# Inputs of the second filter group kept in the filter's buffers, and weight tiles rounded in two halves

## The chip, the cores and the metric

The kernel runs on one core of a Trainium2 chip. The metric is the device time of one execution in microseconds (us); less is better. A core has TensorE (PE, matrix products), VectorE (DVE), ScalarE (ACT) and GpSimd (POOL), which compute, and SyncE (SP), which only issues DMAs here. Each takes its instructions in order: one that waits holds up all that stand behind it on the same engine. DMAs are issued by SP, ACT and POOL.

## The reference

Eight sequences x of 3008 rows and 256 channels go through a filter along the sequence, and its result through a mixer:

```
y  = irfft(rfft(x, axis=1) * (filt_r + 1j * filt_i), n=3008, axis=1)   # float32
h  = relu(y^T @ w_tok1) @ w_tok2            # over the sequence, 256 wide
u  = y + h^T
out = u + relu(u @ w_ch1) @ w_ch2           # over the channels, 1536 wide
```

The mixer's four weights arrive as float64. [...]

## The kernel before

The sequence is split as 3008 = 64 x 47, so that the filter's transforms are matrix products. The batches go in groups: 0, then (1, 2), (3, 4), (5, 6), and 7. For a group, the generator `dft` (line 443) makes first its A units (`a_unit`, line 432): an input of 128 partitions by two rows of 256 is multiplied by a table on PE, ACT copies the result to a tile t1 (two buffers), and ACT issues the DMA that writes it to z in DRAM. The second group has 24 such units, 12 a batch. Each input x comes by two DMAs (`x_load`, line 412) into the pool xp, which has two buffers (XB = 2), so an input is asked for two units ahead. After the A units come the B units (`b_unit`, line 488, and `bi_unit`, line 512): z is read back, multiplied by a table on PE, by the filter on DVE (lines 506 to 510) and by another table on PE. The filter lies in three buffers `filts` (128 x 1024 float32 each), which `filt_load` fills two chunks ahead; they are set to zero once, at the start (line 885), since some of their partitions are never loaded. The generator yields between its steps, and whoever calls `next` decides what stands beside each step.

Rounding. There are 40 weight tiles: 12 of w_tok1, 16 of w_tok2, two early ones of w_ch1 (tiles 28 and 29), and ten late ones, tiles 30 to 39, in the order of LAST (line 373): wc2 0, wc1 1, wc1 4, wc2 1, wc1 2, wc2 2, wc1 5, wc2 3, wc2 4, wc2 5. A tile passes through three steps: its load, by SP or POOL (`begin`); a copy with a factor on ACT (line 250, `copy`); and four DVE operations (lines 252, 253, 255, 257) and the sum of both parts (line 278, `end`). A wc2 tile, and the second wc1 tile of two, is then combined on POOL (`combine`, lines 337 to 344): five operations for a channel pair, the last of which (line 344) writes the form s4. `convert` (line 389) ends one tile, starts the copy of the next, and has POOL issue loads for tiles further on. So ACT's copy is always one tile ahead of DVE.

The mixer (`mix`, line 799) goes through 36 passes for each batch: six blocks m of the sequence by six channel pairs jp. I number the passes of batch 0 from 0. Products of 2 x 2 blocks are made with seven products and extra sums in place of eight products. A pass stands in this order: `convert`; `up_first` (four products on PE, line 693, and a copy s on ACT, line 696); `up_middle` (two DVE sums); the three sums of the pair before (`h_sums`, DVE); `down` part 0 of the pair before (PE, line 727); a yield, place 0, where a step of the filter may stand; `convert`; `up_last` (three products on PE, line 709, then two DVE sums hh, each with a RELU on ACT, line 714); a yield, place 1; `down` part 1; a yield, place 2. All DVE sums of the mixer go through line 671. `up_first` writes the PSUM banks that `up_last`'s sums of the pass before read, so it waits for them. `down` of channel pair jp is made one pass after its `up_last` and needs the combined wc2 tile jp; `up_first` of jp needs the combined wc1 tiles.

The order before pass 0 is written out at lines 886 to 932: batch 0's filter, with the first 12 tiles beside it; then tiles 12 to 27, with two A units of the second group among them; `token_sums(0)` (96 products, line 570); `token_relu`; tiles 28 and 29, each with a `u_unit` (lines 600 and 592); `v_steps`; two more A units; then pass 0. In batch 0 every place takes an A unit until they are all done (20 of them); from then on 35 steps are spread over 48 of the places 1 and 2 (lines 940 to 956). The ten late tiles end in passes 0 to 4, two a pass.

Of the kernel before, what the change touches and what calls it, by code (L numbers as in the profile page):

```python
# [32 lines left out]
XB = 2  # L33
KC = 2
# [90 lines left out]
def kernel(  # L125
# [116 lines left out]
    def halves(st, n, pair):  # L242

        words = [st.bitcast(t).rearrange("p (n w) -> p n w", w=2)[:, 0:n] for t in (U32, FP32)]
        lo, hi, hi_f = words[0][:, :, 0], words[0][:, :, 1], words[1][:, :, 1]
        top, rest = (v[:, 0:n] for v in pair)
        top_i, rest_i = top.bitcast(U32), rest.bitcast(U32)


        nc.scalar.activation(out=top, in_=hi_f, func=AF.Copy, scale=2.0 ** -112)  # L250
        yield
        nc.vector.tensor_scalar(out=top_i, in0=top_i, scalar1=3, scalar2=None, op0=ALU.logical_shift_left)
        nc.vector.scalar_tensor_tensor(out=top_i, in0=hi, scalar=0x80000000, in1=top_i,
                                       op0=ALU.bitwise_and, op1=ALU.bitwise_or)
# [13 lines left out]
    def rounded(st, n, parts, late):  # L268
        if late:

            pair = (p1p.tile([P, 512], FP32, tag="p1", name="top"), p2p.tile([P, 512], FP32, tag="p2", name="rest"))
        else:
            pair = spare_pair()
        h = halves(st, n, pair)
        yield next(h)
        top, rest = next(h)
        for src, dst in parts:
            nc.vector.tensor_tensor(out=dst, in0=src(top), in1=src(rest), op=ALU.add)
# [17 lines left out]
    def w1_load(i):  # L296
# [14 lines left out]
        yield next(h)  # L311
        on_chip(wai_t, *next(h), 512, [(lambda v: v, w1[:, 2 * i:2 * i + 2, :].rearrange("p a t -> p (a t)"))])

    def w2_load(i):
# [15 lines left out]
        if i < BY_PE:  # L330
            h = halves(st, n + more, spare_pair())
            yield next(h)
# [45 lines left out]
    begin, copy, end = iter(tiles), iter(tiles), iter(tiles)  # L378
# [10 lines left out]
    def convert():  # L389

        ended[0] += 1
        while behind and behind[0][0] < ended[0] - 2:
            behind.pop(0)[1]()
        advance(end)
        advance(copy)
        fill(6)
# [13 lines left out]
    xs = {}  # L410

    def x_load(b, c):
# [30 lines left out]
    def dft(bs):  # L443
# [15 lines left out]

        ahead = NXC if first else XB  # L460
        for u in todo[0:ahead]:
            x_load(*u)
        if not first:
            yield True
        for i, u in enumerate(todo):
# [5 lines left out]
            if i + ahead < len(todo):  # L471
                x_load(*todo[i + ahead])
# [57 lines left out]

        for c in range(2):
            t2_load(c)
            if not first:
                w_load(c)
# [264 lines left out]
    def mix(next_ready):  # L799
# [9 lines left out]


# [20 lines left out]
        for i in range(len(items) + 1):  # L831
            now, old = i < len(items), i >= 1
            convert()
            if now:
# [7 lines left out]
                up_middle(hhs[i], w, g, s)  # L842
            one_step()
# [37 lines left out]
    with tc.manual_schedule():  # L881
# [105 lines left out]
```

## Time and profile before

| | |
|---|---|
| four executions | 2570.22, 2571.33, 2572.34, 2575.5 us; median 2571.84 |
| the profiled execution | 2570.22 us, span in the trace 2568.4 us |
| PE busy | 2487.5 us, 97% of the span |
| DVE busy | 1945.3 us, 76% |
| ACT, POOL busy | 660.2 us (26%), 578.0 us (23%) |
| HBM | 168.96 MB read, 77.22 MB written, 96 GB/s over the span |

Where what lies, in us from the start of the span: batch 0's filter ends at about 106; `token_sums(0)` runs from 122.4 to 143.2; pass 0 begins on PE at 154.1 and pass 5 at 212.4; the last A unit of the second group is at 226.8 and its first B unit at 241.8.

How to read the rows: a row of a timeline has the start, the length, the engine, the line of the kernel, the operation, the tile written and the tiles read, the shape, the number of instructions merged into it, and in brackets the idle time of the engine ahead of it with what ended it. The engine ACTq, SPq or POOLq is the part of an engine that issues DMAs. A row of windows has the stretch, its length, the busy time of each engine with the number of instructions, the granted TensorE clock, the DMA engines' share and GB/s.

### The profile page before, as it was taken

Reading aid. Unit: us, or ns where it says so; the run is one execution under the profiler, and the core shown is the slowest. Engines: PE = TensorE matmul, PEld = TensorE weight load, DVE = VectorE, ACT = ScalarE, POOL = GpSimd, SP = SyncE. Lnnn points to the kernel's source line nnn. Section 1 sums busy time; section 2 is a strip of 40 time slices with the busy share of each in tenths; the row PEclk is TensorE's granted clock in tenths of the full one; section 3 lists DMA queues with packets and bytes.
Section 4 is the critical chain, followed back from the end, with each engine's and each line's share of the span. In section 5 each row is a group of like instructions: output and inputs, shape, how many; then the busy total and the mean of one; then the engine's idle time right before and its main releaser. Section 6 shows DMA issues by size and latency. Waiting matters only on the chain.

```text
span 2568.4 us, 32318 instructions
## 1 busy us (share of the span) xinstructions
PE 2487.5 (97%) x11204; PEld 2045.5 (80%) x11204; DVE 1945.3 (76%) x3668; ACT 660.2 (26%) x1312; POOL 578.0 (23%) x1051
## 2 busy tenths in 40 slices
PE   6979999999999999999999999999999999999998
PEld 3557666888888777898888777898888888898887
DVE  7997888566686998756776889856788587757776
ACT  3533222123221222212221222212222122212222
POOL 4563322212111121122121111211211121211222
PEclk8999999999999999999999999999999999999999
DMA  9874444233332332213332333213333222111100
GB/s 211 235 210 147 125 130 140 79 110 102 123 105 78 94 109 74 86 58 109 112 108 86 94 115 97 89 34 110 99 111 90 66 76 71 40 31 37 44 13 20
DMA packets 166932, 248.39 MB, mean 97 GB/s; under 512 B 35184, under 2 KB 112450, under 8 KB 166768
## 3 DMA queue, kind: packets, MB, share of 16 engines
q1 hardware_dynamic: 94176, 152.20, 19.8%
q0 software_dynamic: 32640, 46.51, 7.2%
q10 hardware_dynamic: 39952, 47.61, 5.8%
q8 instruction: 89, 1.46, 0.3%
q14 instruction: 75, 0.61, 0.1%
HBM read 168.96 MB, written 77.22 MB: 96 GB/s over the span
## 4 chain that ended last, share of the span: by engine, by line
PE 70%; DVE 17%; DMA 3%; issue 2%; ACT 2%; SPq 1%; POOL 1%; ACTq 0%; DVEq 0%; POOLq 0%
PE ps_po L727 24%; PE ps_pg L693 14%; PE ps_pg L709 10%; DVE t L671 3%; PE ps_acc L570 3%; DVE hh L671 3%; PE ps_b L614 2%; PE ps_b L570 2%; PE ps_acc L614 2%; DVE u L671 2%; DVE s L671 2%; PE ps_acc L592 2%; PE ps_b L592 2%; PE ps_acc L434 1%; PE ps_acc L518 1%
## 5 line engine op out<-in xcount | busy, mean ns | idle before, releaser
L772 POOL DMA_DIRECT2D out_dram<-r x757 | 410.5, 551 | 1779.8 <-ACT t L524 741.2
L671 DVE TENSOR_TENSOR hh<-ps_pg,s 128x512 f32<-128x512 f32 (+3 forms) x864 | 482.9, 587 | 281.9 <-ACT s L696 271.6
L714 ACT ACTIVATE hh<-hh 128x512 f32<-128x512 f32 (+1 forms) x576 | 348.0, 621 | 1179.7 <-DVE hh L671 1179.7
L727 PE MATMUL ps_po<-t,wc 128*128 128x256 f32 (+1 forms) x2304 | 535.8, 375 | 6.4 <-DVE t L671 5.4
L727 PEld LDWEIGHTS ps_po<-t,wc 128*128 128x128 f32 x2304 | 434.4, 190 | 131.9 <-issue 54.5
L693 PE MATMUL ps_pg<-v,wc 128*128 128x256 f32 (+1 forms) x1728 | 413.7, 375 | 4.1 <-DVE v L671 2.4
L727 PE MATMUL ps_po<-hh,wc 128*128 128x256 f32 (+1 forms) x1728 | 412.8, 375 | 2.1 <-POOL wc L344 1.9
L693 PEld LDWEIGHTS ps_pg<-v,wc 128*128 128x128 f32 x1728 | 326.6, 190 | 45.5 <-DVE v L671 6.4
L727 PEld LDWEIGHTS ps_po<-hh,wc 128*128 128x128 f32 x1728 | 327.7, 190 | 40.4 <-POOL wc L344 2.3
L709 PE MATMUL ps_pg<-u,wc 128*128 128x256 f32 (+1 forms) x1152 | 293.6, 377 | 5.4 <-DVE hh L671 5.1
L671 DVE TENSOR_TENSOR t<-t,hh 128x256 f32<-128x256 f32 (+1 forms) x576 | 244.5, 424 | 19.8
L709 PEld LDWEIGHTS ps_pg<-u,wc 128*128 128x128 f32 x1152 | 216.1, 190 | 42.7 <-DVE hh L671 16.4
L671 DVE TENSOR_TENSOR s<-ps_pg,hh 128x512 f32<-128x512 f32 (+1 forms) x288 | 196.1, 681 | 30.3 <-DVE hh L671 0.5
L671 DVE TENSOR_TENSOR t<-hh 128x512 f32<-128x512 f32 (+1 forms) x288 | 193.4, 672 | 0.6 <-ACT hh L714 0.6
L696 ACT COPY s<-ps_pg 128x256 f32<-128x256 f32 (+1 forms) x288 | 105.8, 367 | 340.5 <-PE ps_pg L693 325.3
L693 PE MATMUL ps_pg<-u,wc 128*128 128x256 f32 (+1 forms) x576 | 168.9, 375 | 0.8 <-DVE hh L671 0.8
L709 PE MATMUL ps_pg<-v,wc 128*128 128x256 f32 (+1 forms) x576 | 168.8, 375 | 0.0
L671 DVE TENSOR_TENSOR u<-ps_b,u 128x512 f32<-128x512 f32 (+3 forms) x111 | 63.5, 572 | 99.5 <-PE ps_b L614 81.0
L671 DVE TENSOR_TENSOR u<-ps_acc,u 128x512 f32<-128x512 f32 (+3 forms) x99 | 57.4, 579 | 95.4 <-PE ps_acc L614 79.2
L693 PEld LDWEIGHTS ps_pg<-u,wc 128*128 128x128 f32 x576 | 109.1, 190 | 23.8 <-issue 10.0
L709 PEld LDWEIGHTS ps_pg<-v,wc 128*128 128x128 f32 x576 | 108.7, 190 | 13.1
L518 PE MATMUL ps_acc<-p,wb 128*96 128x256 f32 (+1 forms) x256 | 97.3, 481 | 12.3 <-ACT t L524 4.5
(123 smaller groups left out, 2514.3 us busy)
## 6 DMA issues: line engine op xcount, KB each, us to landing
w<-w_tmp SPq DMA_DIRECT2D x35, 896.0 KB
g_tmp<-t ACTq DMA_DIRECT2D x128, 192.0 KB
out_dram<-r POOLq DMA_DIRECT2D x698, 32.0 KB, 1.8
x<-in_x_dram SPq DMA_DIRECT2D x173, 128.0 KB
z_tmp<-t ACTq DMA_DIRECT2D x84, 256.0 KB
t<-z_tmp SPq DMA_DIRECT2D x112, 192.0 KB
t<-g_tmp SPq DMA_DIRECT2D x42, 512.0 KB
wb<-wbi_t SPq DMA_DIRECT2D x80, 224.0 KB
```

What stands on the lines that cost most here:

```text
L434: nc.tensor.matmul(ps, wa0 if b == 0 else wa, xs.pop((b, c)).rearrange("p a d -> p (a d)"), start=True, stop=True)
L518: nc.tensor.matmul(ps[0:KR], wbs[k // WC][:, k % WC, P:], p, start=(i == 0), stop=(i == len(parts) - 1))
L570: nc.tensor.matmul(acc[:, t, :], w1[:, a, ts(t, P)], t4[b, a // TC4][:, a % TC4, :], start=(a == 0 and t == 0), stop=(a == A - 1 and t == ...
L592: nc.tensor.matmul(ps[:, ds(q * P, n)], t4[b, c][:, r, ts(dh, P)], wai[:, 0:n], start=(first and q == 0), stop=(not first and q == 3))
L614: nc.tensor.matmul(ps[:, ds(j * hw, hw)], h1[:, n, :], w2m[m % 2][:, at, 0:hw], start=(i < 2 and j == 0), stop=(j == len(todo) - 1))
L671: nc.vector.tensor_tensor(out=out, in0=in0, in1=in1, op=op)
L693: nc.tensor.matmul(ps[:, 0:hw], chan[0][:, jp, n, :], mov, start=True, stop=True)
L696: nc.scalar.copy(out=s[:, 0], in_=g[0][:, 0, 0:hw])
L709: nc.tensor.matmul(ps[:, 0:hw], chan[0][:, jp, n, :], mov, start=True, stop=True)
L714: nc.scalar.activation(out=hs, in_=hs, func=AF.Relu)
L727: nc.tensor.matmul(po[i][:, j, 0:hw], chan[1][:, jp, n, :], mov, start=(jp == 0 and first == 1), stop=(jp == JP - 1 and last == 1))
L772: q.dma_start(rows[g, e, :, ds(h * A + 4 * m, n)], blocks[ts(g, CW), h, e, 0:n])
```

## The change

The second group's A units take their inputs from eight buffers in place of two: of each eight, the first two lie in xp and the other six in the halves of the three `filts`, which nobody uses at that time. Inputs 4 to 9 are issued by POOL, three at tile 22 and three at tile 25; each A unit then loads the next one on SP. After the last A unit POOL sets the three `filts` to zero, ahead of the filter's loads. Four A units (in place of two) stand before pass 0, and they stand right behind `token_relu`, ahead of tiles 28 and 29; two less are left for the passes.

A tile's DVE work is split: the first half is lines 252 and 253, the second lines 255 and 257 and the sum, followed by POOL's combine, the next tile's copy and the loads. Before pass 0 both halves still stand together in `convert`. In a pass, one tile's first half now stands behind `up_middle` and its second half behind `down` part 0; the next tile's first half stands behind place 0, ahead of `up_last`, and its second half behind `up_last`'s sums. `convert` is no longer called at a pass's start.

```diff
+XF = 2 * FB
...
     def halves(st, n, pair):
         nc.scalar.activation(out=top, in_=hi_f, func=AF.Copy, scale=2.0 ** -112)
         yield
         nc.vector.tensor_scalar(out=top_i, ...)
         nc.vector.scalar_tensor_tensor(out=top_i, ...)
+        yield
         nc.vector.tensor_scalar(out=rest_i, ...)
         nc.vector.scalar_tensor_tensor(out=rest, ...)
         yield top, rest
...
     def convert():
-        ended[0] += 1
-        while behind and behind[0][0] < ended[0] - 2:
+        while behind and behind[0][0] < ended[0] - 1:
             behind.pop(0)[1]()
+        advance(middle)
+        convert_end()
+
+    def convert_end():
+        ended[0] += 1
         advance(end)
         advance(copy)
         fill(6)
...
-    def x_load(b, c):
+    def x_load(b, c, i, queue=None):
...
-        t = where.tile([P, xc, dc], FP32, tag=tag, name="x")
+        j = i % (XB + XF) - XB
+        if b in GROUPS[1] and j >= 0:
+            t = filts[j // 2][:, j % 2]
+        else:
+            t = where.tile([P, xc, dc], FP32, tag=tag, name="x")
...
-            q = nc.gpsimd if b == 0 and h else nc.sync
+            q = queue or (nc.gpsimd if b == 0 and h else nc.sync)
...
+        to_load = list(enumerate(todo))
+        def more(n, queue=None):
+            for i, u in to_load[0:n]:
+                x_load(*u, i, queue)
+            del to_load[0:n]
+        more(NXC if first else XB)
+        if bs == GROUPS[1]:
+            ahead.append(more)
...
             a_unit(*u)
-            if i + ahead < len(todo):
-                x_load(*todo[i + ahead])
+            more(1)
...
+        if bs == GROUPS[1]:
+            for t in filts:
+                nc.gpsimd.memset(t, 0.0)
         for c in range(2):
             t2_load(c)
...
+        def late_half(second):
+            if ended[0] < len(tiles):
+                convert_end() if second else advance(middle)
...
         for i in range(len(items) + 1):
-            convert()
             if now:
...
                 up_middle(hhs[i], w, g, s)
+                late_half(False)
             one_step()
             if old:
...
                 down(mo, jo, 0, hhs[i - 1], tts[i - 1], pos.setdefault((bo, mo), []))
             if now:
                 u_parts(b, m, jp, 0)
+            late_half(True)
             yield b, i % n, 0
-            convert()
+            late_half(False)
             if now:
                 up_last(jp, uts[b, m], vts[b, m], w, g, s, hhs[i])
+            late_half(True)
             one_step()
...
             convert()
             if i - rounds < XB:
                 next(second)
+            if i in (A // 2 + TC * N2 // NG - 6, A // 2 + TC * N2 // NG - 3):
+                ahead[0](XF // 2, nc.gpsimd)
             if i == A // 2 + BY_PE - 1:
                 sum_up()
                 acc = token_sums(0)
         h1s[0] = token_relu(0, acc)
+        for _ in range(2 * XB):
+            next(second)
         for dh in range(DH):
             convert()
             u_part(0, 0, dh)
         for f in v_steps(0, 0):
             f()
-        for _ in range(XB):
-            next(second)
```

More of the change, by code (lines that the diff above doesn't have):

```diff
@@ L274, in rounded @@
         h = halves(st, n, pair)
+        yield next(h)
         yield next(h)
@@ L311, in w1_load @@
         yield next(h)
+        yield next(h)
         on_chip(wai_t, *next(h), 512, [(lambda v: v, w1[:, 2 * i:2 * i + 2, :].rearrange("p a t -> p (a t)"))])
@@ L331, in w2_load @@
             h = halves(st, n + more, spare_pair())
+            yield next(h)
             yield next(h)
@@ L377 @@
              + [wc1_load(c * (DC // 512), False) for c in range(DH)] + [f(i) for f, i in LAST])
-    begin, copy, end = iter(tiles), iter(tiles), iter(tiles)
+    begin, copy, middle, end = (iter(tiles) for _ in range(4))
     def advance(it):
@@ L389, in convert @@
     def convert():
+        while behind and behind[0][0] < ended[0] - 1:
+            behind.pop(0)[1]()
+        advance(middle)
+        convert_end()
+    def convert_end():
         ended[0] += 1
-        while behind and behind[0][0] < ended[0] - 2:
-            behind.pop(0)[1]()
         advance(end)
@@ L406, in start @@
         begun[0] += 1
-    xs = {}
-    def x_load(b, c):
+    xs, ahead = {}, []
+    def x_load(b, c, i, queue=None):
         where, tag = ((xp, "x"), (tp, "t"), (vp, "v"), (up, "u"), (t1p, "t1"), (t2p, "t2"))[c // 2] if b == 0 else (xp, "x")
@@ L458, in w_load @@
             filt_load(c, first)
-        ahead = NXC if first else XB
-        for u in todo[0:ahead]:
-            x_load(*u)
+        to_load = list(enumerate(todo))
[6 more added lines that the diff above has]
+            ahead.append(more)
         if not first:
```

## The prediction

> **What bounds the kernel now.** I read the page's slices first, then a table of 10 us windows, then the timelines of PE, DVE, ACT and POOL where PE is not full. In the slices TensorE is at 90% or more in all but the first and the third of 40 slices (64.2 us each); what the change can win lies between 64 and 256 us.
>
> ```profile
> PE   6979999999999999999999999999999999999998
> DVE  7997888566686998756776889856788587757776
> ```
>
> ```profile
> core 0: us, PE busy (x) PEld busy (x) DVE busy (x) ACT busy (x) POOL busy (x), PEclk, DMA share, GB/s
> ...
> 140.00:150.00 10.00, 6.52 (x29) 4.38 (x28) 9.45 (x20) 2.50 (x5) 3.78 (x8) 1.00 0.62 169
> ...
> 160.00:170.00 10.00, 8.32 (x31) 5.57 (x32) 9.07 (x16) 4.38 (x8) 9.15 (x16) 1.00 0.82 254
> 170.00:180.00 10.00, 6.59 (x25) 4.09 (x23) 9.58 (x17) 4.50 (x8) 9.43 (x15) 1.00 0.84 247
> ...
> 210.00:220.00 10.00, 10.00 (x44) 7.40 (x42) 5.42 (x11) 5.19 (x10) 1.50 (x4) 1.00 0.44 142
> ```
>
> From 120 to 210 us DVE is the full engine and PE has holes (granted clock 1.00); from 210 us PE is full and DVE half empty. Now PE's holes:
>
> ```profile
> 147.86 1.12 PE L600 MATMUL ps_acc<-w,h 128*128 128x512 f32 x2 [2.80 <-DVE w L278]
> ...
> 156.45 1.56 PE L693 MATMUL ps_pg<-v,wc 128*128 128x256 f32 x6 [1.73 <-POOL wc L343]
> 158.76 1.10 PE L434 MATMUL ps_acc<-x,wa 128*128 128x512 f32 x2 [0.74 <-DMA x<-in_x_dram]
> ...
> 163.61 1.10 PE L434 MATMUL ps_acc<-x,wa 128*128 128x512 f32 x2 [1.34 <-DMA x<-in_x_dram]
> ...
> 180.19 1.13 PE L727 MATMUL ps_po<-hh,wc 128*128 128x256 f32 x4 [1.94 <-POOL wc L344]
> ...
> 187.77 1.10 PE L434 MATMUL ps_acc<-x,wa 128*128 128x512 f32 x2 [1.71 <-DMA x<-in_x_dram]
> ```
>
> The x waits of this stretch (0.74, 1.34, 0.83, 1.71, 0.72, and 0.37 at 220.67) sum to 5.7 us; those for rounded weights (2.80, 1.73, 1.94) to 6.5. Whether they are worth that depends on DVE, whose own gaps from 155 to 208 us sum to 2.0 us (0.55 at 168.44, 0.61 at 190.89, 0.87 at 203.10). What opens and closes the gap of 0.55:
>
> ```profile
> 163.62 1.28 DVE L671 TENSOR_TENSOR hh<-ps_pg,s 128x512 f32<-128x512 f32 x2
> ...
> 167.19 0.69 DVE L278 TENSOR_TENSOR wc<-top,rest 128x512 f32<-128x512 f32 x1
> 168.44 0.42 DVE L671 TENSOR_TENSOR hh<-ps_pg,s 128x256 f32<-128x256 f32 x1 [0.55 <-ACT s L696]
> ```
>
> ```profile
> 174.50 2.04 POOL L350 DMA_DIRECT2D st<-in_moe_w_ch_dram  x4
> 176.55 0.61 POOL L340 TENSOR_SCALAR wc<-wc 128x128 f32<-128x128 f32 x1
> ...
> 179.36 0.78 POOL L344 TENSOR_TENSOR wc<-wc 128x128 f32<-128x128 f32 x1
> ```
>
> Between the last sums of a pass (hh at 163.62) and the first sums of the next (168.44) lie 4.82 us that ACT needs: two RELUs, the rounding's copy, two copies of the filter's units with their DMA issues, then the copy s. Today a whole weight tile (four operations and the sum, 3.1 to 3.6 us) and the hh sums (1.2) lie in this stretch and all but fill it.
>
> **The change, part by part.** All is counted from the profiled execution (2570.22 us, span 2568.4; 1.6 below the median 2571.84); the sum is a difference, and I add it to the median.
>
> *Filter inputs in filts.* The 24 inputs of the second group are the same DMAs. Twelve issues go to POOL (six inputs, two halves) at 0.62 each, the row of x loads on POOL: 7.4 us among POOL's waits for stage buffers at 134 to 146 us; behind them queue the last weight loads, which have slack: tile 32, issued at 144.52, is copied at 161.06. With eight inputs ahead I drop every x wait. The three memsets (nearest rows: 0.91 for 128x1024 on DVE, 0.52 for 64x512 on POOL) make about 3 us in POOL's 31.46 us of idle before 243.12; on SP the filter loads behind them wait until 231.4 for z anyway. I cost them at nothing; uncovered, 3.
>
> *Four units behind the token sums.* PE is idle from 143.24 to 147.86 but for two matmuls, so 4 x 0.88 = 3.5 us are free there, and the mixer is left with two units fewer: -1.76. But ACT gets four copies with four z writes, and t1 has two buffers: the third copy waits until the first z write has landed, and the rounding's copy of tile 29, both u copies and, through the bank, u_unit wait behind it. That latency has two prices: the unit issued at 154.00 has its packets done by 156.5 (2.4 us, DMA share 0.4 to 0.7), and the one at 166.06 held ACT until 170.90:
>
> ```profile
> 170.90 0.59 ACT L440 COPY t<-ps_b 128x512 f32<-128x512 f32 x1 [2.49 <-DMA z_tmp<-t]
> ```
>
> That is 4.8 us at share 0.8 to 1.0. The six early inputs and four more (2.6 MB) fall on 137 to 150 us, where the share is 0.3 to 0.9 already, so I take 4.8. First unit copied 144.3, its write issued 144.95, landed 149.8; fourth unit copied by 151.5, tile 29 by 153.0; DVE, which takes that tile at 150.61 today, starts 2.4 us late, and so does everything behind it. With 2.4 us instead it is +0.4; with late weight loads behind the x loads too, +4.5. Term: +2.4.
>
> The Trainium skill (DMA: Bandwidth & Descriptors, Issuing engines are not separate DMA queues) says that DMAs started from different engines run on the same 16 engines and interleave, so that another queue saves only issue time. It speaks against moving loads to POOL as a gain. The same page's fit for a POOL DMA (Anatomy of one DMA — SWDGE (gpsimd) path: 2.0 us and bytes over 436e3, for this write 2.6 us as an estimate) would make this term +0.6 instead; the row at 170.90 says otherwise for a loaded moment.
>
> *Rounding in halves.* The count of operations is unchanged. A first half is L252 and L253 (1.18 us, from 160.50 to 161.68), a second L255, L257 and the sum (1.94, to 163.62). In pass 0 the DVE does no whole tile ahead of up_middle: it waits from 155.41 to 157.70 for s, then 1.12 + 1.18 + 2.2 + 1.18 bring the hh sums to 163.4, today 163.62: nothing. From then on each pass pays. Behind the hh sums there is only a second half: 1.2 + 1.94 = 3.1 us to fill the 4.82, so DVE stands 1.7 us where it stood 0 to 0.9; and from up_middle to the next hh sums stand a tile and a half. The gap moves forward what should be behind: +1.2 each pass.
>
> It reaches PE between passes 1 and 2. Pass 1's wc1 tile (two jp, two combines on POOL) is today summed by 167.88; afterwards by 163.4 + 4.82 + 1.12 + 1.18 + 1.55 (sums of the pair before) + 1.94 = 174.0. POOL then needs 6.5 us for two combines (167.98 to 174.50), 2.05 for the loads at 174.50, 3.6 for wc2's combine (176.55 to 180.14): 186.3. Pass 2's down matmuls, which wait for L344, start there, not at 180.19: +6.2. Combines without DVE beside them (2.56 at 209.11) would make it +3.7; all slow ones (3.7) +7.1. I take 6.2, since DVE stays full beside them.
>
> The Trainium skill (SBUF — State Buffer, Who interferes with whom) gives the reason why these lengthen together: a DVE instruction with two SBUF inputs contends with a GpSimd instruction that reads SBUF. The trace agrees: L253 takes 0.69 alone and 0.82 beside a combine. Nothing is added for it.
>
> From there to pass 5's up_first takes 32.2 us today (180.19 to 212.38). Of that 2.4 were x waits, which go; but wc2 tile 3 meets the same queue: two combines of the wc1 tile before it, now summed only 1.2 us ahead of the hh sums, so its combine ends 8.9 us after them and PE, there after 5.6, waits about 3.1. Together +0.7 (between -2.4 and +2.0). Behind pass 5 PE is full, with two units fewer and without the wait of 0.37: -2.1. Later stages move as a whole; the filter's steps start one place earlier, which I cost at nothing.
>
> Sum: 2.4 + 6.2 + 0.7 - 2.1 = +7.2 (ends -0.4 and +11.5), so 2579.0.
>
> **The rivals.** One: the waits simply go. With no DVE wait added, the hh sums of pass 4 (208.94) would come 2.0 (gaps) and 1.9 us (a second half left behind them) earlier, PE's up_first, 2.8 us later than they allow today, would follow at once, and two units are gone: 2.0 + 1.9 + 2.8 + 1.8 = 8.5 us, 2563. For it speaks that PE's holes sum to 13.7 us from 140 to 200; against it ACT's 4.82 us. It decides if ACT's copy s comes within 3.1 us of the hh sums' start, the time that a second half and the sums fill. Two: the halves cost and the inputs pay about alike. If POOL's combines run at 2.56 and the z write at 2.4 us, the sum is 0.4 + 3.7 + 0.7 - 2.1 = +2.7: 2574.5. Three: the inputs were hidden anyway and the halves are hidden too, DVE being full whatever the order: 2572, no change. Four: filter loads behind the memsets come late for the second b unit, where DVE waits 3.25 us for filt at 255.57 already; that would add 3 to 5 us to the sum: 2583.
>
> **How the numbers follow.** This kernel's measurement can tell 0.2% (5.1 us) from no change. My forecast 0.52 (0.08 of it, its low part from 2574 to 2577, inside 0.2%), four 0.11 (slower), two 0.11 and three 0.08 (same), one 0.18 (faster). So faster 0.18, same 0.08 + 0.11 + 0.08 = 0.27, slower 0.44 + 0.11 = 0.55. The likeliest alone: 2574 to 2583.5. The range reaches down until little more than the first rival's 0.18 is left out: 2567 to 2583.5.
>
> **What would show it.** Right: no x wait of PE from 143 to 230; ACT waits for z about 147 to 151; DVE gaps of 1 to 2 us ended by ACT s in passes 1 to 4; a PE wait of 5 us or more for POOL's L344 near 186. Wrong: DVE without gaps there, or PE full from 150. The forecast fails most easily if the two combines do not stand in front of wc2's, since that is 6.2 of the 7.2.

## The result, and the profile after

**A correction first.** The diff above shows the loop of two A units behind `v_steps` as removed. It stays. So eight A units stand before pass 0 (two early ones, four behind `token_relu`, two behind `v_steps`) where four stood, and the passes are left with 16 instead of 20: four units fewer, not two. The prediction was made with this misreading, and one of its terms carries it.

| | before | changed |
|---|---|---|
| median | 2572.48 us (51 executions, 2567.62 to 2577.72) | 2578.21 us (31 executions, 2575.35 to 2580.69) |
| the profiled execution | 2570.22, span 2568.4 | 2578.80, span 2577.0 |

The ratio is 1.0022, 95% interval 1.0017 to 1.0027: slower by 5.7 us, between 4.4 and 6.9. The prediction was 2579.0. The two profiled executions lie 8.6 us apart, since that of before is 2.3 under its median and that of the change 0.6 over. So the differences between these two traces run some 3 us above those between medians.

The slices of the changed kernel:

```profile
PE   6979999999999999999999999999999999999997
DVE  7878888567686998756676889856788587757776
```

TensorE is at 90% or more in the same 37 slices and loses a tenth in the last. DVE is emptier in the second and the third (from 9 to 8 and from 9 to 7) and fuller in the fourth. Nothing here says where 8 us went; the 10 us windows of the changed kernel do (columns as before: stretch, length, busy time of each engine with its instructions, granted clock, DMA share, GB/s):

```profile
core 0: us, PE busy (x) PEld busy (x) DVE busy (x) ACT busy (x) POOL busy (x), PEclk, DMA share, GB/s
140.00:150.00 10.00, 7.80 (x27) 4.59 (x26) 9.48 (x21) 3.54 (x6) 7.76 (x15) 1.00 0.74 210
150.00:160.00 10.00, 9.39 (x30) 4.93 (x29) 5.19 (x9) 3.60 (x6) 3.25 (x6) 0.83 1.03 322
...
180.00:190.00 10.00, 2.89 (x10) 1.65 (x10) 8.15 (x16) 3.79 (x7) 9.29 (x18) 0.89 0.41 131
190.00:200.00 10.00, 9.85 (x29) 6.91 (x30) 5.44 (x10) 3.45 (x6) 2.95 (x6) 0.76 0.63 203
```

Two stretches stand out. From 150 to 160 us DVE, which was the full engine, is busy for 5.19 us only, while the DMA engines are full (1.03). From 180 to 190 PE is busy for 2.89 us. And the granted clock, 1.00 everywhere here in the profiled execution of before, is 0.83, 0.89 and 0.76 in three of these windows. (Other executions of the kernel before have such falls too; see *Is it the clock?*.)

What opens these holes stands in the brackets of the timelines of the changed kernel (idle time ahead of the row, and what ended it). First ACT behind the token sums:

```profile
149.10 0.58 ACT L453 COPY t<-ps_acc 128x512 f32<-128x512 f32 x1 [2.74 <-DMA z_tmp<-t]
154.09 0.58 ACT L453 COPY t<-ps_b 128x512 f32<-128x512 f32 x1 [4.41 <-DMA z_tmp<-t]
155.23 0.67 ACT L251 ACTIVATE both<-st 128x512 f32<-128x512 f32 x1 [0.56 <-DMA st<-in_moe_w_ch_dram]
```

And DVE:

```profile
155.93 0.43 DVE L253 TENSOR_SCALAR both<-both 128x512 uint32<-128x512 uint32 x1 [4.61 <-ACT both L251]
```

The third and the fourth A unit's copies wait for the first and the second z write; tile 29's copy on ACT (L251) stands behind them, and DVE waits 4.61 us for that copy. Then PE's timeline:

```profile
149.73 3.21 PE L622 MATMUL ps_acc<-w,h 128*128 128x512 f32 x4 [2.20 <-ACT t L453]
...
161.59 1.56 PE L715 MATMUL ps_pg<-v,wc 128*128 128x256 f32 x6 [1.75 <-POOL wc L348]
169.30 0.70 PE L715 MATMUL ps_pg<-u,wc 128*128 128x256 f32 x2 [2.27 <-DVE hh L693]
...
180.70 0.70 PE L715 MATMUL ps_pg<-u,wc 128*128 128x256 f32 x2 [1.52 <-DVE hh L693]
190.15 2.07 PE L749 MATMUL ps_po<-hh,wc 128*128 128x256 f32 x4 [6.43 <-POOL wc L349]
...
214.81 1.13 PE L749 MATMUL ps_po<-hh,wc 128*128 128x256 f32 x4 [1.37 <-POOL wc L349]
```

No x wait is left between 143 and 230 us. In their place stand waits for DVE's hh sums and one of 6.43 us for POOL's L349 (L344 before the change), the combine of wc2 tile 1. DVE's own gaps:

```profile
163.03 0.42 DVE L693 TENSOR_TENSOR hh<-ps_pg,s 128x256 f32<-128x256 f32 x1 [2.22 <-ACT s L718]
173.39 0.42 DVE L693 TENSOR_TENSOR hh<-ps_pg,s 128x256 f32<-128x256 f32 x1 [1.61 <-ACT s L718]
184.78 0.42 DVE L693 TENSOR_TENSOR hh<-ps_pg,s 128x256 f32<-128x256 f32 x1 [1.54 <-ACT s L718]
```

One gap a pass, each ended by ACT's copy s: before ACT's copy comes there is too little for DVE to do. And POOL ahead of 190.10 (the first and the last row of a combine of five operations, and the loads between):

```profile
179.08 0.62 POOL L345 TENSOR_SCALAR wc<-wc 128x128 f32<-128x128 f32 x1 [5.82 <-DVE wc L281]
...
181.87 0.97 POOL L345 TENSOR_SCALAR wc<-wc 128x128 f32<-128x128 f32 x1
...
185.08 2.04 POOL L355 DMA_DIRECT2D st<-in_moe_w_ch_dram  x4
187.14 0.55 POOL L345 TENSOR_SCALAR wc<-wc 128x128 f32<-128x128 f32 x1
...
189.58 0.52 POOL L349 TENSOR_TENSOR wc<-wc 128x128 f32<-128x128 f32 x1
```

POOL is idle for 5.82 us until DVE has summed the late wc1 tile (L281, from 178.28 to 178.97); then come two combines of that tile (6.0 us), four DMA issues (2.04), and only then the combine of wc2 that PE needs (3.0).

PE's idle times above 0.25 us in the 110 us behind the token sums add up to 14.0 us before and 18.9 in the changed kernel.

### The profile page after: what moved, and what is told of

Its sections match the earlier page's. It is cut to its first block, busy times and chain, and to the rows that moved or that the text cites. A ratio compares the mean times of both kernels' runs of the same rounds, so it can differ in the third digit from the quotient of the medians.

```text
span 2577.0 us, 32335 instructions
## 1 busy us (share of the span) xinstructions
PE 2492.0 (97%) x11204; PEld 2047.5 (79%) x11204; DVE 1942.2 (75%) x3668; ACT 659.8 (26%) x1312; POOL 583.4 (23%) x1066
## 4 chain that ended last, share of the span: by engine, by line
PE 70%; DVE 19%; DMA 3%; issue 2%; ACT 2%; POOL 1%; ACTq 0%; SPq 0%; DVEq 0%; POOLq 0%
PE ps_po L749 24%; PE ps_pg L715 14%; PE ps_pg L731 10%; PE ps_b L592 4%; DVE t L693 4%; DVE hh L693 4%; PE ps_acc L636 2%; PE ps_acc L592 2%; PE ps_b L636 2%; DVE u L693 2%; DVE s L693 2%; PE ps_b L614 2%; PE ps_acc L614 2%; PE ps_acc L537 1%; DVE p L527 1%
## 5 line engine op out<-in xcount | busy, mean ns | idle before, releaser
L693 DVE TENSOR_TENSOR u<-ps_acc,u 128x512 f32<-128x512 f32 (+3 forms) x111 | 63.4, 572 | 99.9 <-PE ps_acc L636 81.4
L693 DVE TENSOR_TENSOR u<-ps_b,u 128x512 f32<-128x512 f32 (+3 forms) x99 | 57.4, 580 | 95.7 <-PE ps_b L636 79.2
```

What stands on the lines that cost most here:

```text
L693: nc.vector.tensor_tensor(out=out, in0=in0, in1=in1, op=op)
```

## Experiments

The theory: the change has two costs that have nothing to do with each other. **Start:** behind the token sums ACT and POOL bring tile 29's and 30's data late (z writes that hold two t1 buffers; loads that stand in POOL's queue), and pass 0 starts late. **Halves:** splitting the DVE work of a tile (its rounding from float64 to float32) puts the late wc1 tile's end right ahead of wc2's combine on POOL, and PE waits for wc2's behind both combines of that tile, the second of which only the next pass needs. The rivals: the inputs are hidden and only the halves count, or the reverse; the lower clock, not the waits, makes the time; DVE's gaps by themselves make it.

Each kernel was timed in five rounds beside the kernel before; the ratio is to that one. How a trace stands is read from one table, worked out from the traces: the start of `up_first` of a pass, counted from the end of the token sums (143.25 us in the trace of before, 143.82 in that of the change), less the same of before. The zero line is the quick profiled execution of before, and one execution's table carries some 2 us that are not the kernel's: `halves_alone` and `before_late` change nothing ahead of pass 0 and stand at +1.7 there. In both traces the granted clock is 0.50 for 3.4 us just ahead of pass 0 (147.0 to 150.4 and 149.7 to 153.1), which it is not in the trace of before, and the same eight products of a u_unit take 1.86 and 1.92 us there in place of 1.05.

```
                   pass 0      3      4      5      7     36    end
changed              4.54   9.68   9.62  11.04   7.00   7.22   8.00
whole_tiles          3.89   2.14   4.03   4.38   0.34   2.50   3.41
halves_alone         1.68   8.81   8.78  10.21  10.14  10.08   9.60
late_combine         3.82   5.17   5.64   6.47   2.44   2.93   3.31
before_late          1.66   3.80   3.19   3.73   3.59   3.70   3.54
two_units            5.52  10.24  10.21  11.65   9.33  12.19  13.03
two_units_sp         0.15   5.45   5.42   6.85   4.53   7.36   6.77
four_units_sp        9.51  12.91  12.85  14.28  10.24  10.76  10.51
whole_two_sp         0.00   0.34   0.12   0.09  -2.23  -0.28  -0.95
late_two_sp          0.00   1.18   1.68   2.53   0.20   2.14   1.56
whole_late_two_sp    0.02  -2.71  -1.17  -0.67  -2.99  -0.06  -0.59
whole_two_sp_50      0.24  -1.70   0.93   1.66  -0.67   1.37   1.01
filled_hole          4.62   8.78   9.49  10.95   6.91   8.44   7.64
```

### Each part alone

`whole_tiles` is the change without its halves: a whole tile at a pass's start and one ahead of `up_last`, as before.

```diff
             now, old = i < len(items), i >= 1
+            convert()
             if now:
...
-                late_half(False)
             one_step()
...
-            late_half(True)
             yield b, i % n, 0
-            late_half(False)
+            convert()
             if now:
                 up_last(jp, uts[b, m], vts[b, m], w, g, s, hhs[i])
-            late_half(True)
```

> The change without its halves: each weight tile is rounded whole, at the two places that the kernel before has; inputs and early units as in the change. If the halves make the time (through the queue of combines on POOL), the wait of 6.4 us for the combine ahead of pass 2's down matmuls falls to 2 us or less, DVE is full again between passes, and what stays is the late start of DVE (tile 29 about 5 us later) against fewer units in the passes: 2 us faster to 1.5 us slower than the kernel before, so 4 to 7 us under the change. If the early units' z writes make it instead, this kernel stays 4 us or more above the kernel before.

2573.23 us, ratio 1.0007 (0.9998 to 1.0016). PE's wait for the combine is as long as before the change (1.94 there):

```profile
182.26 1.13 PE L749 MATMUL ps_po<-hh,wc 128*128 128x256 f32 x4 [1.95 <-POOL wc L349]
```

`halves_alone` is the kernel before with the halves only: two buffers for x, no loads by POOL ahead, no sets to zero at the end, no four units behind `token_relu`.

```diff
-XF = 2 * FB
+XF = 0
...
-        j = i % (XB + XF) - XB
-        if b in GROUPS[1] and j >= 0:
-            t = filts[j // 2][:, j % 2]
-        else:
-            t = where.tile([P, xc, dc], FP32, tag=tag, name="x")
+        t = where.tile([P, xc, dc], FP32, tag=tag, name="x")
...
-            if i in (A // 2 + TC * N2 // NG - 6, A // 2 + TC * N2 // NG - 3):
-                ahead[0](XF // 2, nc.gpsimd)
...
-        for _ in range(2 * XB):
-            next(second)
```

> The kernel before with the halves alone; inputs in two buffers, units where they were. If the queue of combines makes the time: 5 to 8 us slower than the kernel before, with a PE wait of 5 us or more for the combine's last operation ahead of pass 2's down matmuls, and gaps of DVE of 1 to 2.5 us between the passes that end with ACT's copy s. If the inputs' part makes it: within 2 us of the kernel before.

2578.28 us, ratio 1.0020 (1.0010 to 1.0030): as slow as the whole change. The wait is as long as in the change:

```profile
187.20 2.08 PE L742 MATMUL ps_po<-hh,wc 128*128 128x256 f32 x4 [6.43 <-POOL wc L349]
```

So the halves cost about 5 us, and the inputs part between −0.5 and 4.1. Together these are 0.20% and 0.07%; the change has 0.22%.

### Is it the two combines?

`late_combine` is the change, with the second combine of a late wc1 tile put behind the next wc2 combine. Nothing else moves.

```diff
+    put_off = []
...
         if c == DH - 1:
-            for jp in range(2 * q, 2 * q + 2):
-                combine(chan[0][:, jp:jp + 1])
+            combine(chan[0][:, 2 * q:2 * q + 1])
+            if late:
+                put_off.append(2 * q + 1)
+            else:
+                combine(chan[0][:, 2 * q + 1:2 * q + 2])
...
         combine(chan[1][:, i:i + 1])
+        while put_off:
+            jp = put_off.pop()
+            combine(chan[0][:, jp:jp + 1])
```

> The change with one thing moved on POOL: the second of the two combines of a late wc1 tile stands behind the next wc2 tile's combine. If these two combines in front of wc2's make PE's long wait in pass 2: it falls from 6.4 to about 3.4 us, the wait of 1.4 in pass 4 goes too, and the time falls by 3 to 6 us against the change (the high end if PE's clock then doesn't fall to a half behind the wait). If DVE's gaps make the time: under 1 us.

2573.62 us, ratio 1.0007 (0.9998 to 1.0016). That is 4.6 us under the change's median (3.9 by the ratios), for one combine moved. PE's wait in pass 2:

```profile
185.11 1.20 PE L757 MATMUL ps_po<-hh,wc 128*128 128x256 f32 x4 [2.99 <-POOL wc L349]
```

The wait falls from 6.43 to 2.99, and in the table the jump from pass 0 to pass 3 falls from 5.1 us to 1.4. The later wait, 1.37 in the change, is 0.80 here. DVE's gaps and the halves are all still there; so DVE's gaps in themselves are not the main cost. (Where pass 0 is on time, below, 2.2 us of what the halves cost stay with the combine moved.)

`before_late` puts the same edit into the kernel before.

> The kernel before with the same move of the combines alone. If PE sets the time: up to 1.9 us faster. If DVE and the inputs' transfers set it: no change.

2572.93 us, ratio 0.9997 (0.9988 to 1.0005): no change. PE's wait for the combine goes (1.94 before), but x waits of 3.29 and 3.64 us, longer than the 1.34 and 1.71 of before, stand there (the clock of this trace is 0.50 from 166.8 to 173.6):

```profile
192.56 1.10 PE L442 MATMUL ps_acc<-x,wa 128*128 128x512 f32 x2 [3.64 <-DMA x<-in_x_dram]
```

The order of the combines is worth something only where the halves have made it wrong.

### Why pass 0 starts late

`two_units` has two units behind the token sums in place of four, so that no copy there has to wait for a z write.

```diff
-        for _ in range(2 * XB):
+        for _ in range(XB):
             next(second)
```

> The change with two A units behind the token sums in place of four (six ahead of pass 0 in all, in place of eight). The two buffers t1 then suffice without a wait for a z write there. If that wait delays all that follows: DVE takes tile 29 about 4.5 us earlier, two more units (1.8 us) are left for the passes, and the time falls by 2 to 4 us against the change. If the halves' waits swallow the earlier start: within 1 us of the change, or above it by the two units.

2579.37 us, ratio 1.0027 (1.0016 to 1.0038). The theory's branch failed: the time is not 2 to 4 us under the change, and pass 0 is 5.52 us late instead of 4.54. The time fits the other branch (1.2 us above the change by the medians), but not for its reason, the waits of the halves: the z waits are gone, and the next one is there ahead of pass 0, in ACT's timeline:

```profile
155.14 0.66 ACT L251 ACTIVATE top<-st 128x512 f32<-128x512 f32 x1 [6.08 <-DMA st<-in_moe_w_ch_dram]
```

and in PE's:

```profile
156.33 2.08 PE L447 MATMUL ps_b<-filt,wa 128*128 128x512 f32 x2 [4.43 <-ACT u L625]
```

ACT's copy of tile 30 waits 6.08 us for its load, with the second u copy behind it, and PE waits for that. On POOL the load stands behind six x issues:

```profile
142.44 1.04 POOL L436 DMA_DIRECT2D filt<-in_x_dram  x2
143.71 2.06 POOL L436 DMA_DIRECT2D x<-in_x_dram  x4 [0.24 <-PE ps_b L447]
145.76 0.74 POOL L366 DMA_DIRECT2D st<-in_moe_w_ch_dram  x1
```

New theory: two things hold up tile 29 and 30, the z writes in t1 and the six early inputs on POOL, and either is enough. Then both have to go. `two_units_sp` is `two_units` with the early inputs issued by SP:

```diff
-                ahead[0](XF // 2, nc.gpsimd)
+                ahead[0](XF // 2)
```

> two_units with the six early inputs issued by SP in place of POOL; nothing else. two_units showed the next wait: the load of weight tile 30 was issued by POOL at 145.8 us (139.1 in the kernel before), behind six input loads, landed about 155, and ACT's copy of it held up the second u copy. If POOL's queue is the cause, the load is issued about 6 us earlier, the wait of 6.1 us on ACT goes, pass 0 begins 3 to 5 us earlier against the end of the token sums, and the time falls by 3 to 5 us against two_units. If the load of the DMA engines is the cause (the same bytes at the same time), it stays within 1.5 us.

2576.23 us, ratio 1.0018 (1.0010 to 1.0027). Pass 0 is on time (+0.15). Tile 30's load on POOL:

```profile
142.14 0.74 POOL L366 DMA_DIRECT2D st<-in_moe_w_ch_dram  x1 [1.50 <-DMA x<-in_x_dram]
```

and its copy on ACT:

```profile
150.62 0.68 ACT L251 ACTIVATE top<-st 128x512 f32<-128x512 f32 x1
```

Counted from the end of the token sums (141.80 in `two_units`, 143.32 here), the load is issued 5.1 us earlier, 1.2 before that end in place of 4.0 behind it, and its copy waits for nothing. SP also issues the six inputs earlier than POOL did: the last of them 4.8 us before the end of the token sums (until 138.6), where POOL's last is 4.0 behind it. So the bytes do not move at the same time, as the expectation supposed. But the DMA engines are as full while tile 30's load is under way (a share of 1.04 over 142.1 to 150.3, 1.05 over 145.8 to 155.1 in `two_units`), and it lands after 8.1 us in place of 9.4; so most of what it gains is the earlier issue. The time gained on `two_units` is 2.3 us by the ratios and 3.1 by the medians, where 3 to 5 had been expected: PE's wait for the combine, 7.13 us as in `two_units`, stays.

`four_units_sp` has the inputs on SP and keeps four units.

> The change with the six early inputs issued by SP in place of POOL, and its four units behind the token sums kept: the fourth corner beside the change, two_units and two_units_sp. If either wait ahead of pass 0 alone is enough to hold DVE up (z writes for the third and fourth unit, or tile 30's load), pass 0 still begins 3 to 5 us late against the end of the token sums, with ACT waiting 5 us or more for z writes, and the time stays within 1.5 us of the change. If the loads on POOL were the whole of it, pass 0 begins on time and the time falls by 4 to 5 us.

2579.61 us, ratio 1.0026 (1.0016 to 1.0035), pass 0 late by 9.51, where 3 to 5 had been expected. ACT:

```profile
151.96 0.59 ACT L453 COPY t<-ps_acc 128x512 f32<-128x512 f32 x1 [6.33 <-DMA z_tmp<-t]
```

DVE:

```profile
156.11 0.43 DVE L253 TENSOR_SCALAR both<-both 128x512 uint32<-128x512 uint32 x1 [6.74 <-ACT both L251]
```

So at pass 0: four units and POOL +4.54, two and POOL +5.52, four and SP +9.51, two and SP +0.15. Taking away one cause alone gives nothing; taking away both gives all of it. That four units are worse with SP than with POOL is not explained: the two z writes end ACT's waits 7.6 and 8.6 us after their issue there, against 3.8 and 7.7 in the change, and why isn't shown. A third buffer for t1, which would take the wait from the four units otherwise, was not tried.

### Both parts mended

`whole_two_sp` is `two_units_sp` with whole tiles, `late_two_sp` is `two_units_sp` with the second combine put off, and `whole_late_two_sp` has all three edits.

> The same as two_units_sp, but with the weight tiles rounded whole as in the kernel before: inputs in filts, loads on SP, two units behind the token sums, six ahead of pass 0. If the inputs' part costs only by its two waits ahead of pass 0 (z writes and tile 30's load), both gone here, what is left is the gain: x waits and two units of PE less, 2 to 4 us under the kernel before. If the early inputs' DMA load is what costs, it ends 1 to 3 us above the kernel before.

> two_units_sp with the second combine of a late wc1 tile behind the next wc2 combine, as in late_combine. If the causes add: 4 to 5 us under two_units_sp, and within 2 us of the kernel before. If the earlier start is eaten by another wait, it ends near late_combine (1 to 2 us above the kernel before) or higher.

> whole_two_sp with the second combine of a late wc1 tile behind the next wc2 combine. In whole_two_sp PE still waits 2.5 us for wc2's combine ahead of pass 2's down matmuls (1.9 in the kernel before). If PE sets the time from there: that wait goes, and the time falls by 1.5 to 2.5 us, 3 to 4 us under the kernel before. If DVE sets it (it is full there): under 0.7 us.

| | us | ratio to before |
|---|---|---|
| `two_units_sp` (halves) | 2576.23 | 1.0018 (1.0010 to 1.0027) |
| `late_two_sp` (halves, combine put off) | 2571.65 | 1.0000 (0.9992 to 1.0009) |
| `whole_two_sp` (whole tiles) | 2569.42 | 0.9993 (0.9984 to 1.0001) |
| `whole_late_two_sp` (whole tiles, combine put off) | 2569.19 | 0.9986 (0.9977 to 0.9994) |

With pass 0 on time the halves cost 0.25%, or 6.8 us between the medians, and 4.6 of these go with one combine moved. The inputs without the halves no longer cost anything; the gain of 2 to 4 us that was expected of `whole_two_sp` is 1.6 by the medians, and its interval includes none. The last kernel is faster than the kernel before, by 3.2 us between the medians and between 1.5 and 5.9 by the interval, and so faster than the change too; that it is faster than `whole_two_sp` can't be told from these intervals, and its granted clock is higher too (see *Is it the clock?*). PE's wait for the combine in `whole_two_sp` and in `whole_late_two_sp`:

```profile
181.21 1.31 PE L749 MATMUL ps_po<-hh,wc 128*128 128x256 f32 x4 [2.54 <-POOL wc L349]
```

```profile
177.81 1.13 PE L757 MATMUL ps_po<-hh,wc 128*128 128x256 f32 x4 [0.28 <-POOL wc L349]
```

These two rows do not show what the moved combine brings. `whole_two_sp_50` (below), which is the same kernel as `whole_two_sp` up to its B steps, waits 0.26 us at this place, without the move:

```profile
181.02 1.13 PE L749 MATMUL ps_po<-hh,wc 128*128 128x256 f32 x4 [0.26 <-POOL wc L349]
```

In its trace the clock is 0.50 from 177.0 to 180.4, ahead of the wait; in that of `whole_two_sp` it is 0.50 from 182.0 to 185.4, behind the wait. Pass 3 stands at −1.70 in the one and at +0.34 in the other. And what is gained in `whole_late_two_sp` does not stay: −2.71 at pass 3, −0.67 at pass 5. PE's idle times behind the token sums add up to 12.5 us there, against 14.0 before.

All kernels with two units behind the token sums gain 2.3 us from pass 5 to pass 7, as two units fewer and the wait of 0.37 should give (2.1), and lose 1.9 to 2.9 again by pass 36; `whole_tiles` loses 2.2, the change 0.2. Two things stand in the traces. Where the loss is 2.8 or 2.9, and in `whole_tiles`, the clock is 0.50 once for 3.4 us in that stretch (from 473.0 in `two_units`, 469.8 in `two_units_sp`, 461.1 in `whole_late_two_sp`, 238.6 in `whole_tiles`); in the other traces of this paragraph it is not, and the loss is 1.9 or 2.0 with two units. And PE's waits for DVE's product p of B units in that stretch sum to 5.5 us before and 6.3 in the change, but to 8.2 in `two_units` and `whole_two_sp`. The first of them in `whole_two_sp`:

```profile
243.44 1.10 PE L537 MATMUL ps_acc<-p,wb 128*96 128x512 f32 x2 [1.50 <-DVE p L529]
```

One reason for these waits could be where the filter's steps stand, which start earlier when the A units end earlier. `whole_two_sp_50` spreads the 35 steps over 50 places:

```diff
-left, places, at, spread = K2 + 3, 2 * 24, 0, True
+left, places, at, spread = K2 + 3, 2 * 25, 0, True
```

> whole_two_sp with its 35 B steps spread over 50 places in place of 48. It is 2.2 us ahead of the kernel before where the A units end and only 0.3 ahead when batch 0 ends: its B steps begin two places earlier. If that gain is lost because the steps stand closer than DVE can take them: 1 to 2 us faster than whole_two_sp. If it is lost by how the steps meet the passes: within 1 us either way.

2570.18 us, ratio 0.9991 (0.9983 to 1.0000), and in its trace 2.0 us are given back as well, from −0.67 to 1.37. The spread is not shown to be the reason: the wait of 1.50 us is there as well, and the waits for p sum to 6.8 us. So the 2 us that two units fewer win are lost again beside longer waits for p; why these are longer stays open.

### Is it the clock?

Around the wait of 6.43 us the clock falls. Windows of the changed kernel:

```profile
core 0: us, PE busy (x) PEld busy (x) DVE busy (x) ACT busy (x) POOL busy (x), PEclk, DMA share, GB/s
185.00:187.50 2.50, 0.00 (x0) 0.00 (x0) 2.36 (x5) 0.31 (x1) 2.43 (x6) 1.00 0.69 207
187.50:190.10 2.60, 0.00 (x0) 0.00 (x0) 2.50 (x5) 0.00 (x0) 2.36 (x6) 0.58 0.23 84
190.10:194.30 4.20, 4.15 (x8) 2.67 (x9) 2.27 (x4) 0.33 (x1) 1.54 (x2) 0.50 0.56 177
194.30:197.00 2.70, 2.70 (x11) 1.97 (x10) 1.68 (x4) 1.24 (x3) 0.00 (x0) 0.92 0.85 294
```

The four down products at 190.15 take 2.07 us; the same row takes 1.13 at 214.81. `filled_hole` puts seven idle products into the wait, so that PE stays busy.

```diff
+                if i == 2:
+                    idle = bank(free_bank())
+                    for _ in range(7):
+                        nc.tensor.matmul(idle, wa, w1[:, 0:2, :].rearrange("p a t -> p (a t)"), start=True, stop=True)
                 tts[i - 1] = tp.tile([P, 4, 256], FP32, tag="t", name="t")
```

> The change with seven products more on PE (128x512 each, into a bank that nobody reads; 6.0 us) ahead of pass 2's down matmuls, where PE waits 6.4 us for the combine. They do no work for the result. In the change the granted clock falls to 0.5 for 6.8 us behind this wait, 4.2 us of which PE works. If the idle time itself brings the clock down: no stretch at 0.5 there, and 1.5 to 2.5 us under the change. If the clock falls for another reason: within 0.7 us of the change or slower.

2576.13 us, ratio 1.0017 (1.0009 to 1.0026), against 1.0022 (1.0017 to 1.0027) of the change: these intervals neither show nor exclude the gain of 1.5 to 2.5 us. The clock did stay up there. Windows of `filled_hole`, then PE's timeline:

```profile
183.00:190.00 7.00, 6.11 (x16) 2.60 (x14) 5.54 (x10) 1.34 (x3) 6.58 (x12) 1.00 0.45 150
190.00:193.00 3.00, 2.75 (x11) 2.06 (x12) 1.87 (x3) 0.59 (x1) 1.69 (x3) 1.00 0.42 85
```

```profile
182.40 6.28 PE L875 MATMUL ps_acc<-w,wa 128*128 128x512 f32 x14
...
190.25 1.13 PE L749 MATMUL ps_po<-hh,wc 128*128 128x256 f32 x4 [1.15 <-POOL wc L349]
```

The products take 1.13 us again, and from the end of wc2's combine (190.20, and 190.10 in the change) to pass 5 it takes 32.46 us in place of 33.89: the fall costs 1.4 us in the change's trace. The table hides this (10.95 and 11.04 at pass 5), because two other things are slower in the trace of `filled_hole`: its clock is 0.50 from 163.7 to 167.1 (pass 1 starts 0.6 later), and wc2's combine takes 3.66 us on POOL in place of 2.96.

So a fall of the clock on the path cost 1.4 us here and 1.7 in the table's pass 0. Does it make the 5.7? The mean granted clock of every execution is on record: 0.9930 on average over the 104 executions of the kernel before that were timed beside the experiments, 0.9927 over those of the change. A thousandth of the span is 2.6 us, so this difference is worth 0.8 us at most. The executions at 0.993 take 2572.1 us on average in the kernel before (52 of them) and 2578.1 in the change (14). So the clock is not what makes the change slower; falls belong to the kernel before as well, and its profiled execution (0.995) has fewer than most. But the clock makes part of the scatter: the kernel before takes 2574.1 us at 0.992 (22 executions), 2572.1 at 0.993 and 2570.7 at 0.994 (21). And the two smaller gains above have a higher clock with them: 0.9943 in `whole_two_sp` and 0.9948 in `whole_late_two_sp`, against 0.9931 and 0.9929 of the kernel before beside them. At 1.7 us a thousandth, an estimate from the first and the last of the three averages, that is 2.0 and 3.2 us, about all of their gain; whether these kernels bring the higher clock themselves, by fewer waits, isn't shown.

What such a fall looks like without any change of the kernel there: `halves_alone` ahead of pass 0, and PE's row in it (1.05 us in the trace of before):

```profile
147.00:150.40 3.40, 3.40 (x10) 2.37 (x11) 3.23 (x7) 0.00 (x0) 0.00 (x0) 0.51 0.01 1
```

```profile
148.78 1.86 PE L607 MATMUL ps_acc<-wai,t 128*128 128x128 f32 x8
```

## Why the prediction came out right

Its terms, against the trace of the change (differences counted from the end of the token sums, those of the combines from the end of wc2 tile 1's combine, 190.10 against 180.14):

| step | predicted | measured |
|---|---|---|
| four units behind the token sums: pass 0 starts late | +2.4 (+0.4 to +4.5) | +4.5 |
| halves: two combines ahead of wc2's | +6.2 (+3.7 to +7.1) | +4.85 |
| from there to pass 5 | +0.7 (−2.4 to +2.0) | +1.65 |
| fewer units, the wait of 0.37 gone (pass 7) | −2.1 | −4.0 |
| sum | +7.2 | +7.0 at pass 7 |

By the medians it is +5.7. The mechanisms of the two main terms were right, the sizes of all four terms were off, and the errors balanced: that the sum came so close is luck. (A slip of reading without weight: the last of the 40 slices is under 90% as well, not only the first and the third.)

*Four units behind the token sums* was at the end of its range. The prediction priced the z write at 4.8 us, from the row at 170.90. Issued at 145.34 and 146.39 us, the first write had landed by 149.10 (3.8 us) and the second by 154.09 (7.7). The error is that one price was used for both writes, while they overlap and the DMA engines are full there. Its other end, +4.5, was for late weight loads as well; `two_units` shows that these were late too, hidden behind the z waits. The prediction gave them slack by the row of tile 32; tile 30, two tiles ahead, had none (issued at 147.69 in the change, landed 8.8 us later, copied at 156.49).

*Two units fewer* (−1.76) is the misreading of the code: it is four, and 4 x 0.88 and the wait of 0.37 make −3.9; the trace has −4.0.

*The two combines*: the theory carries, by `halves_alone` and `late_combine`. The late wc1 tile was forecast to be summed at 174.0, without the late start; with that (4.5, and 0.6 for the token sums) 179.1, and the trace has 178.97. Too high was the price of the combines: 6.0 us for two and 3.0 for wc2's, where 6.5 and 3.6 had been taken from rows with a full DVE beside them. Here DVE had gaps, which the same text forecast. (In `filled_hole` wc2's took 3.7; so DVE alone need not set this price.) *To pass 5*: the second wait, for wc2 tile 3, was forecast at 3.1 us and took 1.37, and the x waits of 2.4 went as forecast; by that the term would be −1.0. It is +1.65. Some 1.4 of it is the clock, which the prediction had nowhere: in `filled_hole`, where it stays at 1.00 behind the combine, the term is +0.22. The rest may be there because the end of the x waits brought nothing forward: from pass 3 to pass 4 the table stays at 9.7 and 9.6. DVE stands idle there for 2.85 us until PE's late products (at 195.28; 1.24 in `filled_hole`) and for 2.12 until ACT's s (2.91), and the next pass waits for its sums. That this is what used up the 2.4 us is argued from the rows and no run shows it by itself.

What was to be seen: no x wait of PE from 143 to 230 (none); ACT's waits for z about 147 to 151 (they end at 149.10 and 154.09); DVE gaps of 1 to 2 us ended by ACT s in passes 1 to 4 (1.61, 1.54, 2.12, 2.31, and 2.22 in pass 0); a wait of 5 us or more for L344 near 186 (6.43, ended at 190.15).

The rivals: *the waits simply go* fell with ACT's copy s, which sets DVE's gaps as the prediction said. *The halves cost and the inputs pay alike*: the inputs do not pay; they cost nothing only where pass 0 is on time (`whole_two_sp`). *All hidden anyway* falls with `halves_alone`. *Filter loads late*: the three sets to zero take 0.93 to 0.95 us each, from 225.53 to 229.0, and DVE's wait of 3.25 us for filt at 255.57 is gone. One of 4.08 us for filt stands at 267.96, where DVE waited 4.38 for PE before the change (267.04), and PE's wait there is 0.68 in both: the 3 to 5 us of this rival did not come. PE's wait of 1.97 us for p, at 246.83, is longer than any for p in that trace of before (1.27); no term had it.

## What to carry to other kernels

When work on an in-order engine is cut in halves, ask for each piece which wait it now stands behind, and what queues behind its end on the next engine: here a tile that ended some 6 us later put two combines, one of them for the next pass only, ahead of the one that PE was waiting for, and moving a single combine won back 4.6 of the 6.8 us. If taking away one cause of a delay changes nothing, a second one may be hidden behind it: mending both put pass 0 4.4 us forward, mending one put it 1 to 5 us back. And read a loop that is "moved" in the whole file, not in the diff's lines alone. Last, before two traces are compared by a microsecond or two, look for falls of the granted clock in both: one of 3.4 us moved pass 0 by 1.7 us here in kernels that had changed nothing ahead of it.

## What was unexpected of the hardware

*The clock.* The granted clock falls to 0.50 and stays there for some microseconds: about 187.9 to 194.7 in the changed kernel, by the windows above, and from 150.4 to 153.8, behind a hole of only 2.20 us. Windows of the changed kernel:

```profile
147.50:149.70 2.20, 0.04 (x1) 0.00 (x0) 2.10 (x6) 0.58 (x1) 2.20 (x5) 1.00 0.99 275
149.70:153.00 3.30, 3.27 (x6) 1.47 (x7) 1.56 (x3) 0.00 (x0) 1.25 (x3) 0.60 1.05 346
```

A longer hole in `before_late`, of 3.64 us, leaves it at 1.00:

```profile
188.90:192.60 3.70, 0.06 (x2) 0.07 (x1) 3.60 (x8) 1.70 (x3) 2.96 (x6) 1.00 0.98 289
192.60:196.00 3.40, 3.40 (x14) 2.64 (x15) 1.55 (x3) 1.53 (x3) 2.58 (x5) 1.00 0.86 236
```

The Trainium skill (TensorE: Matmul & The Clock Gate, Part 1: The HAM clock gate) says that the clock is halved after an idle window of about 3.4 us and that these windows run freely. The hole of 3.64 us agrees, since such a hole need not cover a whole window. The hole of 2.20 us can't cover one, and the clock fell behind it all the same: PE was busy for 1.20 of the 3.40 us from 146.9 to 150.3. Behind a hole of 2.82 us in `halves_alone` (at 146.96) it fell too, and behind the hole of 2.80 us at the same place in the trace of before it did not.

*A queue's order is more than issue time.* The Trainium skill (DMA: Bandwidth & Descriptors, Issuing engines are not separate DMA queues) says that starting DMAs on another engine saves only the issue time. Between `two_units` and `two_units_sp` the same bytes are loaded, only the issuer of six inputs differs (and with it the time of their issue), and pass 0 moves by 5.4 us. The six issues right ahead of tile 30's load take 3.1 us (1.04 and 2.06); the load itself is issued 5.1 us later on POOL and lands 6.4 later, counted from the end of the token sums. What adds the 2.0 us to the issues isn't shown; POOL's order has more in it than their length.

*A z write under load.* The same 256 KB took 2.4 us in the kernel before at a DMA share of 0.69 (154.0 to 156.5) and 4.8 at 0.98 (166.0 to 170.9), 3.8 and 7.7 us in the change at 0.99 and 1.01, and 7.6 and 8.6 in `four_units_sp` at 1.05 and 1.01. So the share alone does not tell how long a write takes.
